# Seven products of 256 columns in place of eight, in five of the eight MLP blocks

## The chip, the cores and the metric

The kernel runs on one core of one Trainium2 chip. The metric is the device time of one execution in microseconds (us). An execution here is one call on the whole input: 2048 tokens, both layers.

## The reference

Two layers, each with a linear-attention block and an MLP, on one sequence of S = 2048 tokens with D = 448 features; 16 heads of 28; hidden size F = 1792. All in float32.

```python
x = x + A(layernorm(x), wqkv, wo)      # phi(q), phi(k) = where(t > 0, t + 1, exp(t)) + 1e-6
                                       # o = phi(q) @ (phi(k).T v) / (phi(q) . sum phi(k) + 1e-6), then @ wo
x = x + (gelu(layernorm(x) @ w1 + b1) @ w2 + b2)
# both lines twice, with the same weights
```

The change touches the product `layernorm(x) @ w1` (2048 x 448 times 448 x 1792) and what feeds it.

## The kernel before

**Precision.** Every large product is made in the type fp32r from split operands: a float32 value is written as hi + lo, and a product takes three matmuls, hi x hi, hi x lo and lo x hi. Of the 448 input features, 384 make three full chunks of 128 rows; the last 64 are laid twice into one chunk, so that hi and lo of the weight stand above one another, and need two matmuls in place of three. A product over all features thus takes 3 x 3 + 2 = 11 matmuls.

**Stages.** Each layer has a first phase over 16 tiles of 128 tokens (layer norm, projections to k and q, sums for attention), a short middle part, and four blocks of 512 tokens. A block goes over 14 chunks i of 128 hidden features. For each, `mlp1` makes the product with w1 (11 matmuls of 512 tokens, L1011), then gelu on ScalarE (L1013), the cast to hi on ScalarE (L1016) and the low part on VectorE (L1017). `mlp2` (L1040 to L1042) multiplies gelu's hi and lo with w2: four token tiles times three matmuls of 448 columns, added up in four PSUM banks over all 14 chunks; then VectorE adds the sum to x (L1045) and SP stores it (L1047).

**Order.** All instructions stand in an order written by hand; each engine runs its own in order. `mlp1` of chunk i + 1 stands ahead of `mlp2` of chunk i, and of the next block's first chunk ahead of the last `mlp2`. Between them `behind` puts the preparation of the next block: the tuples `PLAN_0`, `PLAN_1` and `PLAN` name for each chunk which steps go there. Tokens: `ld`, `g` loads; `z`, `p`, `q`, `o` the attention output of one token tile (`o` is `oc_mm`, L948 to L952, 11 matmuls, and `o_ln`, L969 and the layer norm's statistics); `n` the normalisation and a transpose in 32x32 squares on VectorE (L308); `sx` and `lx` a way through DRAM that completes the transpose; `x` (`m_part`, L354 and L355) the split of a piece of the MLP's operand, the cast on ScalarE and the low part on VectorE.

**Buffers.** w1 and w2 are split once, hi and lo, and stay in SBUF: `w1h`, `w1l`, `w1x`, `w2h`, `w2l`. They are loaded and split piece by piece in layer 0 (`bg_pieces`, `background`: cast on ScalarE, L419, L422, L430; low part on GpSimd, L420, L423, L431), w1 and four chunks of w2 during the first phase and the rest of w2 during the first block. The transposed operand of a block lies in XH and XL, two buffers each. PSUM has eight banks: "h" (2) for hp, "acc" (4) for the sums of `mlp2`, "m" (2) for op and others.

**Queues.** Nearly all DMAs are issued by SP, in program order; where one waits, those behind it wait too.

Of the kernel before, what the change touches and what calls it, by code (L numbers as in the profile page):

```python
# [22 lines left out]
def linear_attn_mlp_kernel(  # L23
# [22 lines left out]
    NG = D // G  # L46
    TL = D - 64
    LAYERS = 2

# [151 lines left out]
    w2l = wts.tile([128, NF, D], F32R, name="w2l")  # L201

# [29 lines left out]

    class Block:
        def __init__(self, key):
            at = APART if key[0] == "a" else 0
            self.rows = key[0] == "m"
            self.hi = work.tile([128, 2048], F32R, name="XH", tag="XH", bufs=2)
            self.lo = work.tile([128, 2112], F32R, name="XL", tag="XL", bufs=2)[:, at:at + 2048]

        def pieces(self, t):  # L240

            if self.rows:
                return tuple(x.rearrange("p (c t n) -> p t c n", c=4, t=4)[:, t] for x in (self.hi, self.lo))
            s = slice(t * 512, (t + 1) * 512)
            return self.hi[:, s], self.lo[:, s]

        def moving(self, x, c):

            return x[:, c * 512:(c + 1) * 512]

        def still(self, x, t, c):

            return x[:, (t * 4 + c) * 128:(t * 4 + c + 1) * 128]
# [71 lines left out]
    def half_square(name, j):  # L325

        if j >= 2:
            return t512("AB"[j - 2], 2, name)
# [8 lines left out]
    def turn_one(x, key, j):  # L337
# [4 lines left out]
                      x[:, TL:D].rearrange("p (m n) -> p m n", n=32)[:, None].to_broadcast([128, 2, 2, 32]))  # L342

# [19 lines left out]
    def proj(name, key, j, o=None, cs=range(4), at=(3, 6, 9, 11)):  # L363
# [3 lines left out]
        if len(cs) == 4:  # L367
            w = [wkq[name, c] for c in range(3)]
            his = [(b.still(b.hi, j, c), p) for c in range(3) for p in w[c]] + [(b.still(b.hi, j, 3), wkq[name, 3])]
            los = [(b.still(b.lo, j, c), w[c][0]) for c in range(3)] + [(b.still(b.lo, j, 3), wkq[name, 3])]  # L370
# [3 lines left out]
        for c in cs:  # L374
            if c < 3:
                hi, lo = wkq[name, c]
                pe.matmul(o, b.still(b.hi, j, c), hi, start=(c == 0), stop=False)
                pe.matmul(o, b.still(b.hi, j, c), lo, start=False, stop=False)
                pe.matmul(o, b.still(b.lo, j, c), hi, start=False, stop=False)
            else:  # L380
                pe.matmul(o, b.still(b.hi, j, 3), wkq[name, 3], start=False, stop=False)
                pe.matmul(o, b.still(b.lo, j, 3), wkq[name, 3], start=False, stop=True)
# [11 lines left out]

    def bg_pieces():
        n = 0
        both = []

        def stage():
            nonlocal n  # L400
            n += 1
            if n <= LATE:
                k = (n - 1) // 2
                if k % 2 == 0 or k > 5:
                    return t512("xn", 2, "stg")[:, :D]

                if n % 2:
                    both.append(half("stg"))
                return both[-1][:, n % 2 * 512:][:, :D]
            return t448(f"W{5 + n % 2}", 1, "stg")  # L410

        for fc in range(4):
            sl = slice(fc * D, (fc + 1) * D)
            for c in range(4):
                s = stage_piece(w1[:, sl], c, sp, stage())

                def go(c=c, s=s, sl=sl):
                    if c < 3:
                        act.copy(w1h[:, c, sl], s)  # L419
                        pool.tensor_tensor(w1l[:, c, sl], s, f(w1h[:, c, sl]), op=OP.subtract)  # L420
                    else:
                        act.copy(w1x[:, sl], s)  # L422
                        pool.tensor_tensor(w1x[64:128, sl], s[64:128], f(w1x[64:128, sl]), op=OP.subtract)  # L423
                yield go
        for i in range(NF):
            s = stage()
            sp.dma_start(s, w2[i * 128:(i + 1) * 128, :])

            def go(i=i, s=s):
                act.copy(w2h[:, i], s)  # L430
                pool.tensor_tensor(w2l[:, i], s, f(w2h[:, i]), op=OP.subtract)  # L431
            yield go
# [4 lines left out]
    def background(n, m=NF):  # L437

        for g in bg_wait[:m]:
            bg_wait.pop(0)()  # L440
        for _ in range(n):
            g = next(bg, None)
            if g is not None:
                bg_wait.append(g)


# [45 lines left out]
    def stage_s(l, t):  # L492
        xn = xns.pop((l, t))
        h = t512("A", 2, "xnh", F32R)
        lo = t512("B", 2, "xnl", F32R, APART)
# [81 lines left out]
    def product(name, t, c, p):  # L577
# [8 lines left out]
        pe.matmul(o, b.still(b.lo if p == "l" else b.hi, t, c), w, start=(n == 0), stop=(n == 11))  # L586
# [57 lines left out]
    def stage_g(l, t, acc, mid=lambda: None):  # L644
# [618 lines left out]
```

## Time and profile before

| what | value |
|---|---|
| median of 3 runs | 864.18 us (864.15 to 867.68) |
| profiled execution | 864.72 us |
| its span | 863.0 us |
| busy: TensorE, its weight loads | 857.2 us (99%), 768.1 us (89%) |
| busy: VectorE, ScalarE, GpSimd | 493.0, 352.8, 211.6 us |
| matmuls in L1011 | 1232 of 512 columns |
| moved by DMA | 97.89 MB |

The span is the time between the first and the last instruction that the profiler recorded. Busy times of TensorE's rows overlap, since its instructions are pipelined: the mean duration of a matmul is longer than the distance between two starts. "acc", "h" and "m" are names of PSUM banks, not columns of the profile.

### The profile page before, as it was taken

The numbers are of one execution on the slowest core, as the hardware profiler recorded it, in microseconds if no ns is written. First come the engines' busy times: TensorE is split into PE (matmuls) and PEld (weight loads), VectorE is DVE, ScalarE is ACT, GpSimd is POOL, SyncE is SP. The second block draws the span as 40 slices with busy tenths as digits, with TensorE's granted clock in tenths as the row PEclk, the third lists the DMA queues.
The fourth block names the chain that finished last, engine by engine and source line by source line (L and its number), as shares of the span: only waits on it lengthen the run. The fifth ranks groups of instructions, "written<-read, shape, count | busy, mean of one in ns | idle before, by whom it ended". The sixth has DMA issues, their size and how long they took to land.

```text
span 863.0 us, 11715 instructions
## 1 busy us (share of the span) xinstructions
PE 857.2 (99%) x4155; PEld 768.1 (89%) x4155; DVE 493.0 (57%) x962; ACT 352.8 (41%) x635; POOL 211.6 (25%) x244
## 2 busy tenths in 40 slices
PE   9999999999999999999999999999999999999998
PEld 8999988888888888888899998988888888888887
DVE  7888586559456443236477876764664383533112
ACT  7676655323323322333356565633232233233231
POOL 3576612235013012012222343120310140140000
PEclk9999999999999999999999999999999999999999
DMA  5485647633313402051146442462332423111001
GB/s 171 150 270 180 206 108 217 191 113 121 123 61 123 140 0 98 1 182 49 49 150 188 164 130 96 146 204 81 123 113 78 140 74 111 49 49 43 1 1 43
DMA packets 68681, 97.89 MB, mean 113 GB/s; under 512 B 9488, under 2 KB 62864, under 8 KB 68624
## 3 DMA queue, kind: packets, MB, share of 16 engines
q1 hardware_dynamic: 67872, 96.76, 35.0%
q8 instruction: 32, 0.52, 0.3%
q10 hardware_dynamic: 752, 0.41, 0.2%
q14 instruction: 25, 0.20, 0.1%
HBM read 57.74 MB, written 36.18 MB: 109 GB/s over the span
## 4 chain that ended last, share of the span: by engine, by line
PE 90%; DVE 4%; DMA 3%; issue 1%; ACT 1%; POOL 1%; SPq 0%; DVEq 0%; ACTq 0%; POOLq 0%
PE hp L1011 32%; PE y L1041 10%; PE y L1040 10%; PE y L1042 10%; PE psq L372 5%; PE G L658 5%; PE psk L372 5%; PE op L949 2%; PE op L948 2%; PE op L950 2%; DMA sp<-sq_a 1%; PE op L938 1%; PE op L937 1%; PE op L939 1%; PE kvp L824 1%
## 5 line engine op out<-in xcount | busy, mean ns | idle before, releaser
L1017 DVE TENSOR_TENSOR gl<-g,gh 128x512 fp32r<-128x512 f32 x112 | 83.2, 743 | 293.0 <-ACT gh L1016 293.0
L1013 ACT ACTIVATE g<-hp,b1s 128x512 f32<-128x512 f32 x112 | 77.1, 689 | 400.8 <-PE hp L1011 400.8
L1041 PE MATMUL y<-w2l,gh 128*128 128x448 f32 x447 | 163.6, 366 | 0.0
L1040 PE MATMUL y<-w2h,gh 128*128 128x448 f32 x447 | 162.0, 362 | 0.0
L1042 PE MATMUL y<-w2h,gl 128*128 128x448 f32 x447 | 160.0, 358 | 0.0
L1011 PE MATMUL hp<-XH,w1h 128*128 128x512 f32 x336 | 130.7, 389 | 0.0
L1011 PE MATMUL hp<-XH,w1l 128*128 128x512 f32 x336 | 130.7, 389 | 0.0
L1011 PE MATMUL hp<-XL,w1h 128*128 128x512 f32 x336 | 130.1, 389 | 0.0
L216 POOL TENSOR_TENSOR brs<-bve,mhalf 128x1 f32<-128x1 f32 x55 | 34.2, 622 | 258.5 <-DVE bve L215 250.8
L1040 PEld LDWEIGHTS y<-w2h,gh 128*128 128x128 f32 x447 | 83.7, 187 | 9.4
L1041 PEld LDWEIGHTS y<-w2l,gh 128*128 128x128 f32 x447 | 83.9, 188 | 7.0
L1042 PEld LDWEIGHTS y<-w2h,gl 128*128 128x128 f32 x447 | 84.0, 188 | 5.0
L1011 PEld LDWEIGHTS hp<-XL,w1h 128*128 128x128 f32 x336 | 63.1, 188 | 13.1
L1011 PEld LDWEIGHTS hp<-XH,w1h 128*128 128x128 f32 x336 | 63.0, 187 | 10.7
L1011 PEld LDWEIGHTS hp<-XH,w1l 128*128 128x128 f32 x336 | 63.1, 188 | 9.9
L1016 ACT CAST gh<-g 128x512 fp32r<-128x512 f32 x112 | 69.6, 621 | 3.6
L372 PE MATMUL psk<-wk,XH 128*128 128x448 f32 x210 | 61.8, 364 | 0.0
L372 PE MATMUL psq<-wq,XH 128*128 128x448 f32 x196 | 57.0, 365 | 0.0
L497 POOL TENSOR_TENSOR xnl<-x,xnh 128x384 fp32r<-128x384 f32 x32 | 35.0, 1094 | 73.5 <-ACT xnh L496 60.3
L355 DVE TENSOR_TENSOR XL<-sp,XH 128x512 fp32r<-128x512 f32 x58 | 47.2, 825 | 5.7 <-ACT XH L354 5.7
L883 POOL TENSOR_TENSOR pz<-pq,zb 128x448 f32<-128x448 f32 x24 | 28.2, 1174 | 89.9 <-DVE dn L894 61.8
L658 PE MATMUL G<-kh,xnh 128*128 128x448 f32 x128 | 46.7, 367 | 0.0
(194 smaller groups left out, 1500.2 us busy)
## 6 DMA issues: line engine op xcount, KB each, us to landing
x<-in_A_x_dram SPq DMA_DIRECT2D x32, 224.0 KB, 3.9
pq_d<-eq SPq DMA_DIRECT2D x32, 224.0 KB, 2.5
pq<-pq_d SPq DMA_DIRECT2D x32, 224.0 KB, 3.6
x<-x_d SPq DMA_DIRECT2D x32, 224.0 KB, 3.9
sq_a<-sq SPq DMA_DIRECT2D x13, 512.0 KB, 2.9
sp<-sq_a SPq DMA_DIRECT2D x52, 128.0 KB, 2.9
sq_q<-sq SPq DMA_DIRECT2D x12, 512.0 KB, 2.6
sp<-sq_q SPq DMA_DIRECT2D x48, 128.0 KB, 2.8
```

The lines of the kernel that those rows point to most:

```text
L216: pool.tensor_tensor(rs, ve, mhalf, op=OP.pow)
L355: eng.tensor_tensor(lo.rearrange("p c (i n) -> p c i n", n=32), x, f(h), op=OP.subtract)
L372: pe.matmul(o, x, p, start=(i == 0), stop=(i == 10))
L497: pool.tensor_tensor(lo[:, :TL], xn[:, :TL], f(h[:, :TL]), op=OP.subtract)
L658: pe.matmul(acc[c], w, k, start=first and c not in others[0], stop=last and c not in others[1])
L1011: pe.matmul(hp, w, r, start=(k == 0), stop=(k == len(made) - 1))
L1013: act.activation(g, hp, AF.Gelu_apprx_tanh, bias=b1s[:, i:i + 1])
L1016: act.copy(gh, g)
L1017: dve.tensor_sub(gl, g, f(gh))
L1040: pe.matmul(acc[j], gh[:, s], w2h[:, i], start=first, stop=False)
L1041: pe.matmul(acc[j], gh[:, s], w2l[:, i], start=False, stop=False)
L1042: pe.matmul(acc[j], gl[:, s], w2h[:, i], start=False, stop=stop)
```

## The change

In five of the eight blocks (the third and fourth of layer 0, the second to fourth of layer 1) the product with w1 is made by Strassen's scheme in Winograd's form. A block's 512 tokens are halved, the features are halved (two chunks each) and a pair of hidden chunks is halved: eight products of quarter size become seven, of sums. The operand's sums S1 to S4 are made by GpSimd in place in the transposed tiles and then split like any piece (seven pieces a block in place of four). Products 1, 6, 7 and 4 add up in one bank of "h", 5 and 3 in one half of a bank of "m", 2 in its other half; ScalarE copies three of them to SBUF on the way, and VectorE adds three times. Products 1, 5, 6 and 7 take six matmuls of 256 columns, 2, 3 and 4 take five.

The sums of w1 are made once, in layer 0's first blocks (`seven_pair`: four subtractions and an addition on GpSimd, casts on ScalarE, low parts on VectorE, 13 DMAs a pair of chunks). w1's split parts no longer stay in SBUF: all blocks, the three old ones too, fetch them from DRAM, pair by pair, into two tiles with two buffers each. XH and XL become rings of nine pieces. The other three blocks keep their 11 matmuls of 512 columns; their operand is now read in four stretches of 128. `mlp2`'s matmuls are the same in number and shape, in another order.

```diff
+    SEVEN = {(0, 2), (0, 3), (1, 1), (1, 2), (1, 3)}
...
-    w1h = wts.tile([128, 3, F], F32R, name="w1h")
-    w1l = wts.tile([128, 3, F], F32R, name="w1l")
-    w1x = wts.tile([128, F], F32R, name="w1x")
...
+    def fetch_a(p, seven=True):
+        w = w1a[seven, p] = work.tile([128, 12 * 128], F32R, name="w1a", tag="w1a", bufs=2)
+        if seven:
+            sp.dma_start(f(w[:, :512]), w1c_d[p][:, :512])
+            sp.dma_start(f(w[:, 512:]), w1t_d[p][:, :1024])
+        else:
+            sp.dma_start(f(w[:, :1024]), w1c_d[p][:, :1024])
+
+    def fetch_b(p, seven=True):
+        w = w1b[seven, p] = work.tile([128, 13 * 128], F32R, name="w1b", tag="w1b", bufs=2)
+        sp.dma_start(f(w[:, :768]), w1c_d[p][:, 1024:])
+        if seven:
+            sp.dma_start(f(w[:, 768:]), w1t_d[p][:, 1024:])
...
+    def seven_pair(p):
...
+        pool.tensor_tensor(t1, t3, t1, op=OP.subtract)
+        pool.tensor_tensor(t3, t2, t3, op=OP.subtract)
+        yield
+        pool.tensor_tensor(t2, t2, t1, op=OP.subtract)
+        pool.tensor_tensor(t4, t4, t2, op=OP.subtract)
+        yield
+        high = temp("th", F32R)
+        act.copy(high, top)
...
-        (0, 5): "qp K s kp X kh v9 a10 kl n10 G bg Q ld sp",
+        (0, 5): "qp K s kp X kh v9 a10 kl n10 G sp bg Q ld",
...
+    PRODUCTS = {1: ("a", (0, 1, 2, 3), "A11"), 5: ("a", (4, 6, 5, 7), "S1"), 6: ("a", (8, 10, 9, 11), "S2"),
+                2: ("b", (0, 4, 2), "A12"), 3: ("b", (1, 5, 3), "S4"), 7: ("b", (6, 8, 7, 9), "S3"), 4: ("b", (10, 12, 11), "A22")}
...
+        def product(self, n):
+            w, at, name = PRODUCTS[n]
...
+            made = [(u[0], h[0]), (u[1], h[0]), (u[0], x[0])]
+            made += [(u[2], h[1]), (u[3], h[1]), (u[2], x[1])] if n in (1, 5, 6, 7) else [(u[2], h[1]), (u[2], x[1])]
+            if n in (1, 6, 7, 4):
+                first = n == 1
+                self.X = bank("h", 2, "hx") if first else self.X
+                o = self.X[:, :256]
+            else:
+                first = self.HB is None
+                self.HB = bank("m", 2, "hy") if first else self.HB
+                o = self.HB[:, 256:] if n == 2 else self.HB[:, :256]
...
+        def keep_2(self):
+            self.s2 = self.small("s2")
+            act.copy(self.s2, self.x())
...
+        def c12(self):
+            dve.tensor_tensor(self.s2, self.s2, self.y(), op=OP.add)
+
+        def rest(self):
+            self.gelu(21, self.x())
+            self.gelu(12, self.s2)
+            self.high(12)
+            self.high(21)
+            self.low(12)
+            self.low(21)
...
     LATER = (
         "n3 sx1 ld1 ld2",
         "lx1 ld3 z0",
-        "x0 p0 z1",
-        "x1 p1 sq0 z2",
-        "x2 p2 z3 lq0",
-        "x3 p3 sq1",
-        "",
-        "lq1",
+        "p0 z1",
+        "c1 c3 p1 sq0 z2",
+        "x0 x1 p2 z3 lq0",
+        "c2 c4 p3 sq1",
+        "x2 x3 x4",
+        "x5 lq1",
     )
...
+    def step(l, b, k, tr):
+        c = todo.pop(0)
+        n = len(ahead) - len(todo) + 1
+        before = open_.pop(0)
+        q = quarters(before)
+        c.product(1)
+        c.keep_1()
+        if (before.l, before.b) not in SEVEN:
+            q[0]()
+            c.product(2)
+            c.c11()
+            c.product(6)
+            c.keep_2()
+            c.product(5)
+            c.keep_5()
+        else:
+            c.product(5)
+            c.keep_5()
+            before.rest()
+            q[0]()
+            c.product(2)
+            c.c11()
+            c.product(6)
+            c.keep_2()
+        fetch(held_a, fetch_a, n)
...
+        if k == 0:
+            token_piece(l, b, 6)
+        c.g11()
+        q[1]()
+        c.product(7)
+        c.c22()
+        c.low(11)
...
+        beside(l, b, 2 * k, tr)
+        q[2]()
...
+        q[3]()
+        c.low(22)
+        c.product(3)
+        c.product(4)
+        c.c12()
+        beside(l, b, 2 * k + 1, tr)
...
+        fetch(held_b, fetch_b, n)
+        open_.append(c)
```

A step is one pair of chunks: its seven products stand between the four quarters of the pair before it (11, 22, 12, 21 by token half and hidden half, six matmuls of 448 columns each). `beside` calls `behind` with the plan's tokens for the step's two chunks; `c1` to `c4` are the operand's sums, `x0` to `x5` its pieces. `more`, left out, takes `seven_pair` one `yield` further; it is called in layer 0's first three blocks.

More of the change, by code (lines that the diff above doesn't have):

```diff
@@ L392, in phi @@
         return into
-    def bg_pieces():
[L396 to L424, printed above, removed]
-        for i in range(NF):
[L426 to L432, printed above, removed]
@@ L447, in linear_attn_mlp_kernel, with sevens @@
+    def sevens():
+        for p in MADE:
+            yield from seven_pair(p)
+        yield
+    seven = sevens()
     xns, split, ks = {}, {}, {}
@@ L701, in linear_attn_mlp_kernel @@
     PRE = 5
-    BG = [0, 1] + [2] * 6 + [1] * 7 + [0]
-    LATE = sum(BG)
     loaded = {0: 3}
@@ new lines, in linear_attn_mlp_kernel, with fetch, quarters @@
+    todo, open_ = [Pair(*c) for c in ahead], []
+    held_a, held_b = ([(False, 0), (False, 1)] for _ in range(2))
+    def fetch(held, get, n):
+        if n < len(ahead):
+            l, b, p = ahead[n]
+            key = ((l, b) in SEVEN, p)
+            if key not in held:
+                get(p, key[0])
+                held.append(key)
+                del held[0]
+    def quarters(c):
+        if (c.l, c.b) not in SEVEN:
+            return [lambda i=i, js=js: mlp2(c.l, c.b, i, js) for i, js in
+                    ((NF - 2, range(4)), (NF - 1, (0, 1)), (NF - 1, (2, 3)), (NF - 1, ()))]
+        first, last = (c.p == turn_of(c.l, c.b)[i] for i in (0, -1))
+        return [lambda q=q: quarter(c, q, first, last) for q in (11, 22, 12, 21)]
@@ L1132, in linear_attn_mlp_kernel, with last_step @@
+    def last_step():
+        while open_:
+            c = open_.pop(0)
+            c.rest()
+            for q in quarters(c):
+                q()
     table(AF.Exp)
```

520 lines of the change are left out of this document (404 added, 116 removed), and 6 rows, old and new, of tables (ORDER, STEPS).

## The prediction

> **What bounds the kernel now.** I read the page's busy table and its slices first, then TensorE's matmuls grouped by line and shape, then single matmuls in order of time, then the windows that fit the blocks, and last the groups of ScalarE, VectorE and GpSimd.
>
> ```profile
> span 863.0 us, 11715 instructions
> PE 857.2 (99%) x4155; PEld 768.1 (89%) x4155; DVE 493.0 (57%) x962; ACT 352.8 (41%) x635; POOL 211.6 (25%) x244
> PEclk9999999999999999999999999999999999999999
> PE 90%; DVE 4%; DMA 3%; issue 1%; ACT 1%; POOL 1%; SPq 0%; DVEq 0%; ACTq 0%; POOLq 0%
> L1011 PE MATMUL hp<-XH,w1h 128*128 128x512 f32 x336 | 130.7, 389 | 0.0
> L1011 PE MATMUL hp<-XH,w1x 128*128 128x512 f32 x112 | 43.6, 389 | 0.0
> 286.30:363.60 77.30, 77.30 (x367) 68.62 (x366) 28.37 (x54) 22.71 (x36) 7.68 (x8) 1.00 0.19 63
> 788.30:859.40 71.10, 71.10 (x338) 62.74 (x337) 14.13 (x23) 18.34 (x28) 0.00 (x0) 1.00 0.04 15
> ```
>
> TensorE is the clock of this kernel: 99% busy, 90% of the chain, full clock in every slice, and no idle time before any L1011 group. In the two windows, which are two of the eight MLP blocks (layer 0's third, layer 1's last; in the columns PE, PEld, DVE, ACT, POOL, clock, DMA share, GB/s), the other engines are busy for 8 to 29 of 71 to 77 us. So what the change is worth is first a sum over matmuls, and what one costs is the distance between starts, since busy times overlap.
>
> ```profile
> 599.81 0.39 PE L1011 MATMUL hp<-XH,w1h 128*128 128x512 f32 x1
> ...
> 602.30 0.36 PE L948 MATMUL op<-wq,qh 128*128 128x448 f32 x1
> ```
>
> ```profile
> 788.31 0.39 PE L1011 MATMUL hp<-XH,w1h 128*128 128x512 f32 x1
> ...
> 790.81 0.36 PE L1040 MATMUL y<-w2h,gh 128*128 128x448 f32 x1
> ```
>
> ```profile
> 854.82 0.36 PE L1042 MATMUL y<-w2h,gl 128*128 128x448 f32 x1
> ...
> 858.62 0.26 PE L1032 MATMUL yh<-w2h,gh 128*128 128x224 f32 x1
> 858.72 0.28 PE L1033 MATMUL yh<-w2l,gh 128*128 128x224 f32 x1
> ...
> 859.17 0.27 PE L1034 MATMUL yh<-w2h,gl 128*128 128x224 f32 x1
> ```
>
> Eleven 512-wide matmuls take 2.49 us in one place and 2.50 us in the other: 4.99 / 22 = 226.8 ns each. Nineteen 448-wide take 3.80 us: 200 ns. The difference, 26.8 ns for 64 columns, is 0.42 ns a column, and the line through both has a fixed part of about 13 ns. The 224-wide ones at the very end start 0.45 / 4 = 112.5 ns apart in their steady part, where the line would give 106.
>
> **The first product, term by term.** A pair of feature chunks takes 2 x 11 = 22 matmuls of 512 columns today. The scheme's seven products take 4 x 6 + 3 x 5 = 39 matmuls of 256. Five blocks of seven pairs are 35 pairs: 770 wide matmuls leave (770 x 0.2268 = 174.6 us), 1365 narrow ones come. No group of 256 columns is in the trace. The line gives 200 - 192 x 0.42 = 119.4 ns, and I take 120. The low bound is the 112.5 ns of the 224-wide row, as if that were a floor below which no width matters; the high bound is that row plus 32 columns, 112.5 + 13.4 = 126 ns. I stay with 120 because 112.5 looks like a second limit, the weight load's, which these rows show:
>
> ```profile
> 858.73 0.19 PEld L1034 LDWEIGHTS yh<-w2h,gl 128*128 128x128 f32 x1
> ...
> 858.84 0.19 PEld L1032 LDWEIGHTS yh<-w2h,gh 128*128 128x128 f32 x1
> ...
> 859.07 0.19 PEld L1034 LDWEIGHTS yh<-w2h,gl 128*128 128x128 f32 x1
> ```
>
> Loads of 0.19 us start 0.11 us apart, so they overlap, and one matmul per 0.113 us (0.34 / 3) is what they allow; 120 is above it, so the columns decide again. The sum: 1365 x 0.120 = 163.8, a gain of 10.8 us. At 112.5 it is 153.6 and 21.0; at 126 it is 172.0 and 2.6. The change breaks even at 174.6 / 1365 = 127.9 ns. All depends on 8 ns a matmul.
>
> The Trainium skill speaks against the change here: "Perfetto Trace Analysis", Identifying the Most-Contended Engine, says that weight loads' busy share, not matmul's, tells how near TensorE is to its limit. By it the 595 more loads at 188 ns would add 112 us to a row that is 89% busy, more than the span has room for. The three load rows above contradict this, since they overlap.
>
> The second product keeps its count: a pair was 2 x 12 matmuls of 448 and is four quarters of 6. Its cost stays 24 x 0.200 = 4.8 us, and a step of the new loop is 39 x 0.120 + 4.8 = 9.5 us, against 9.8.
>
> **What has to hide in a step.** ScalarE and VectorE get more and shorter instructions.
>
> ```profile
> L1013 ACT ACTIVATE g<-hp,b1s 128x512 f32<-128x512 f32 x112 | 77.1, 689 | 400.8 <-PE hp L1011 400.8
> L1016 ACT CAST gh<-g 128x512 fp32r<-128x512 f32 x112 | 69.6, 621 | 3.6
> L281 ACT CAST XH<-tp 128x512 fp32r<-128x512 f32 x4 | 2.3, 572 | 0.9 <-PE tp L269 0.9
> L290 ACT CAST XH<-tp 128x256 fp32r<-128x256 f32 x4 | 1.4, 368 | 0.1
> L1017 DVE TENSOR_TENSOR gl<-g,gh 128x512 fp32r<-128x512 f32 x112 | 83.2, 743 | 293.0 <-ACT gh L1016 293.0
> L292 DVE TENSOR_TENSOR XL<-tp,XH 128x256 fp32r<-128x256 f32 x4 | 1.6, 422 | 0.4 <-ACT XH L290 0.2
> ```
>
> Halving a ScalarE copy from 512 to 256 columns saves 572 - 368 = 204 ns. So a pair's ScalarE work goes from 2 x (689 + 621) = 2.6 us to three kept products (368 each), four gelus (689 - 204 = 485) and four casts (621 - 204 = 417): 4.7 us of 9.5. VectorE goes from 1.5 to 7 x 0.42 = 3.0 us. Neither is a bound; their order is what counts. The tightest place: product 7 adds onto the bank that keep_2 has to copy first. Between product 6 and product 7 stands one quarter, 6 x 0.200 = 1.2 us. On ScalarE's queue ahead of keep_2 are keep_1, keep_5 and, once the loop runs, the two gelus and two casts of the pair before: 2 x 368 + 2 x 485 + 2 x 417 = 2.5 us. Product 1 ends at 0.72 us in the step and product 6 at 0.72 + 0.72 + 1.2 + 0.6 + 0.72 = 3.96. A matmul's result is there about 0.17 us after its slot (366 ns shown against 200). Started at about 0.9, with a wait for product 5, ScalarE is through by about 3.9; keep_2 runs to some 4.6 and product 7 is due at 5.16. It holds with 0.5 us over. I cost it at nothing; without that margin each 0.1 us late costs 35 x 0.1 = 3.5 us.
>
> **Stalls that I do cost.** First, the products' other bank comes from the same two banks as attention's output op. Where two of these fall in one step (o0 and o1, o2 and o3), the second needs the bank that c12 still reads, and c12 stands on VectorE behind the first one's chain.
>
> ```profile
> L210 DVE BATCH_NORM_STATS2 bst<-x 128x6 f32<-128x448 f32 x4 | 2.5, 628 | 0.1
> L969 DVE TENSOR_TENSOR x<-op,x 128x448 f32<-128x448 f32 x4 | 2.5, 624 | 0.6
> L308 DVE STREAM_TRANSPOSE sq<-xm 128x384 f32<-128x384 f32 x4 | 2.3, 578 | 0.1
> L228 DVE TENSOR_SCALAR xm<-x,bmv,brs 128x448 f32<-128x448 f32 x4 | 2.0, 504 | 0.0
> ```
>
> These four with about half a microsecond of small ones and low22 (0.42) make 3.3 us, against two quarters and products 3 and 4, 2.4 + 1.2 = 3.6. With c12's own 0.42 the second op is 0.2 to 0.7 us late: 0.45 in each of two steps in three blocks (those that prepare another), 2.7 us; bounds 0 and twice that.
>
> Second, each of the two passages from an old block to a new one: ScalarE there has one gelu and one cast (1.3 us), four operand pieces (4 x 0.62) and then keep_1, some 4.3 us after the last wide matmul, while product 6 is due after product 1, twelve second products and product 2, 0.72 + 2.4 + 0.6 = 3.7. I take 0.8 us twice, 1.6; bounds 0 and 4.
>
> At the layers' ends the last pair's gelus and casts need about 2.2 us under two quarters of 2.4; nothing there. The operand's three more pieces a block and four sums on GpSimd (below 1.4 us each by the row below) lie behind blocks where these engines are idle for over half of the time.
>
> **Layer 0 and the DMA.** Weights of the first product no longer stay in SBUF.
>
> ```profile
> q1 hardware_dynamic: 67872, 96.76, 35.0%
> 30.00:60.00 30.00, 30.00 (x152) 27.82 (x152) 26.71 (x57) 21.70 (x43) 20.61 (x25) 1.00 0.65 209
> 134.00:145.00 11.00, 11.00 (x52) 9.50 (x51) 6.08 (x12) 6.05 (x10) 2.75 (x2) 1.00 0.79 250
> 156.00:167.00 11.00, 11.00 (x53) 9.76 (x53) 6.23 (x10) 4.59 (x8) 3.29 (x3) 1.00 0.77 221
> L883 POOL TENSOR_TENSOR pz<-pq,zb 128x448 f32<-128x448 f32 x24 | 28.2, 1174 | 89.9 <-DVE dn L894 61.8
> ```
>
> 96.76 MB in 35.0% of 863 us is 320 MB per ms of full use, so the 25 blocks of 64 KB (1.6 MB) that a pair fetches are 5.1 us of DMA in a step of 9.5 to 10.3, some 50% beside the 0.19 of the block in the first fence: about 0.7, and each fetch is issued a whole step ahead. SP is held at a fetch until product 6 or 4 has read the old tile; what queues behind it is the next plan's loads, of a later step. It is tighter in layer 0: 6.4 MB of stores in the first phase (20 us of DMA over some 84, on top of 0.65), and in the first block, at 0.77 to 0.79 for its first 33 us, three fetches and the first sums' transfers, 3 to 4 MB or about 11 us more. That reaches 100%, so loads land a few microseconds late. Behind them on ScalarE stand casts of pieces, and behind these the gelus; the two banks of hp cover about 2.5 us of that. Bounds 0 to 8 us; I take 0.7, since those loads are planned two chunks (over 10 us) ahead.
>
> **Sum.** 864.7 (the profiled execution, 1.7 over its span) - 10.8 + 2.7 + 1.6 + 0.7 = 858.9. The median shown is 0.5 lower, so I expect 858.4.
>
> **Rivals.**
> (1) All is hidden: 864.2 - 10.8 = 853.4. For it: no idle time before L1011 today. Against: the shared bank. Chance 0.17.
> (2) The forecast, 855.5 to 859.8: 0.38.
> (3) No change, 860 to 868: the price is 125 to 126 (a gain of 2.6 to 4.0, eaten by the stalls: 864.2 - 3.3 + 5 = 865.9), or the DMA of layer 0 takes its upper 8 us (858.4 + 7.3 = 865.7). Chance 0.29.
> (4) Slower: keep_2 gates product 7. It decides as soon as ScalarE is later than its margin by (10.8 + 4.3) / 35 = 0.43 us a step, that is 0.9 us later than my count. At 0.9 us of stall a step: 858.4 + 31.5 = 890; at 0.6, 879. For it: in-order ScalarE stands in the step's middle with seven instructions and can be held by a late transfer or sum. Against: 4.7 us of work in 9.5. Chance 0.12.
> (5) The floor of 112.5 ns holds at 256 columns: 858.4 - 10.2 = 848. "TensorE: Matmul & The Clock Gate" in the Trainium skill, Back-to-back issue gap, would have N / 2.4 + 2.5 = 109 ns, thus 1365 x 0.109 = 149 and a gain of 26. The 448- and 512-wide rows, 11 ns above that rule each, speak against it. Chance 0.03.
> (6) Weight loads don't overlap at this width: 1365 x 0.188 = 256.6, time 858.4 + 92.8 = 951. The yh rows speak against it; 0.01.
>
> **The numbers.** Changes under 0.5%, 4.3 us, can't be told from none. Faster, below 859.9: 0.17 + 0.38 + 0.03 = 0.58, less 0.02 for stalls near the border, 0.56. Slower, above 868.5: 0.13 with (6), and 0.01 from the end of (3), 0.14. Same 0.30. The range goes from 851.5, a little under the full gain, to 867, where the first half of (3) and the DMA case end; the likeliest case's own is 855.5 to 859.8.
>
> **What would show it.** Narrow matmuls 119 to 121 ns apart inside a product; 0.2 to 0.7 us of TensorE idle ahead of every second op; short idles at product 6 of the first pair; none at product 7; DMA at 0.6 to 0.8 in the new blocks. Wrong would be: over 124 ns, idle before product 7 in most steps, or tens of microseconds of idle in layer 0's first 240 us.

## The result, and the profile after

The changed kernel takes 907.25 us (median of 4 runs, 904.54 to 910.5) beside 864.36 us for the kernel before (864.15 to 867.68): the ratio is 1.0488, with a 95% interval from 1.044 to 1.0537. It is 4.9% slower. The profiled execution took 904.54 us, 1.7 us over its span.

From the page of the changed kernel: span, busy times, the granted clock in 40 slices, the DMA queue, the chain by engine, and one group of the narrow matmuls (busy us, mean ns, idle us before it and what ended it).

```profile
span 902.8 us, 13895 instructions
...
PE 867.3 (96%) x4750; PEld 795.4 (88%) x4750; DVE 573.0 (63%) x1180; ACT 428.8 (47%) x907; POOL 269.6 (30%) x304
...
PEclk9999899989999979999999999999999999999999
...
q1 hardware_dynamic: 112894, 179.15, 61.4%
...
PE 75%; DMA 9%; DVE 8%; SPq 3%; ACT 2%; issue 2%; POOL 1%; DVEq 0%; ACTq 0%; POOLq 0%
...
L1174 PE MATMUL hx<-XH,w1a 128*128 128x256 f32 x280 | 53.8, 285 | 0.6 <-ACT s L1190 0.6
```

TensorE's share of the chain fell from 90% to 75%; DMA rose from 3% to 9%, VectorE from 4% to 8%. The queue moved 179.15 MB in place of 96.76. The clock has three slices below 9. So matmuls no longer set the end everywhere; windows tell where. From the windows of the changed kernel (stretch, length, then busy us and count of PE, PEld, DVE, ACT, POOL, the granted clock, the DMA share, GB/s):

```profile
60.00:104.00 44.00, 34.28 (x146) 29.94 (x145) 25.03 (x52) 20.67 (x38) 18.53 (x26) 0.88 0.71 238
...
175.00:186.00 11.00, 7.34 (x34) 6.01 (x32) 2.69 (x7) 3.10 (x6) 3.98 (x6) 0.96 0.92 274
186.00:197.00 11.00, 9.39 (x34) 7.83 (x35) 6.90 (x12) 3.18 (x6) 4.23 (x4) 0.73 0.87 261
...
312.00:330.00 18.00, 13.30 (x62) 11.74 (x61) 12.70 (x20) 7.85 (x17) 8.69 (x7) 0.72 0.67 207
...
396.00:475.00 79.00, 79.00 (x504) 75.40 (x503) 47.34 (x107) 44.44 (x105) 13.88 (x15) 1.00 0.67 221
...
592.00:620.00 28.00, 25.28 (x118) 21.73 (x116) 17.29 (x34) 9.53 (x16) 4.62 (x4) 1.00 0.85 256
...
671.00:690.00 19.00, 17.32 (x110) 15.88 (x109) 14.04 (x27) 11.26 (x26) 3.47 (x3) 1.00 0.67 236
```

Once the new blocks run (396 to 475) TensorE is full. It is idle in the first phase, in the first block, at the first entry into a new block (312 to 330), in layer 1's first block (592) and at the second entry (671).

The first phase ends with the first kvp matmul. Its row in the view of that tile (duration ns min/median/max, first and last start) says 104.3 us in the kernel before and 122.9 in the changed one:

```profile
L824 PE MATMUL kvp<-gt,stg x64: 258/262/262, 104.3 to 532.0; 128*112 128x112 f32 x64
```

```profile
L934 PE MATMUL kvp<-gt,stg x64: 258/262/263, 122.9 to 565.9; 128*112 128x112 f32 x64
```

The table is made the same way, from starts of single matmuls: a block runs from its first matmul with w1 to the next one's. "Stall" adds up, over a stage, how much the distances between starts exceed 200 ns after a 448-wide matmul, 226.7 after 512 and 120 after 256; in the kernel before it is 1.7 us in the first phase and 0.0 in every block. (The eight matmuls on `mp` in each layer's middle part are left out of it. At each of the two passages from an old block to a new one 12 second products change sides of the mark, 2.4 us, so of the stages on both sides of a passage only the stall compares.)

| stage | before, us | after, us | stall after, us |
|---|---|---|---|
| first phase, layer 0 | 104.3 | 122.9 | 20.3 |
| layer 0: first, second block (old) | 75.0, 77.4 | 83.7, 75.4 | 8.8, 0.5 |
| layer 0: third block (new) | 77.4 | 84.8 | 9.6 |
| fourth (new) and the next first phase | 165.3 | 166.2 | 1.1 |
| layer 1: first block (old) | 75.0 | 78.1 | 5.6 |
| layer 1: second, third, fourth (new) | 77.4, 77.4, 70.9 | 79.9, 76.4, 72.0 | 4.7, 1.3, 0.8 |

All stalls come to 54.0 us against 3.3: with 10.8 us less of matmuls, 54.0 - 3.3 - 10.8 = 39.9, and the last matmul starts 898.9 - 859.2 = 39.7 us later.

### The profile page after: what moved, and what is told of

The parts are those of the page before. It is cut to its first block, busy times and chain, and to the rows that moved or that the text cites. A ratio compares the mean times of both kernels' runs of the same rounds, so it can differ in the third digit from the quotient of the medians.

```text
span 902.8 us, 13895 instructions
## 1 busy us (share of the span) xinstructions
PE 867.3 (96%) x4750; PEld 795.4 (88%) x4750; DVE 573.0 (63%) x1180; ACT 428.8 (47%) x907; POOL 269.6 (30%) x304
## 3 DMA queue, kind: packets, MB, share of 16 engines
q1 hardware_dynamic: 112894, 179.15, 61.4%
## 4 chain that ended last, share of the span: by engine, by line
PE 75%; DMA 9%; DVE 8%; SPq 3%; ACT 2%; issue 2%; POOL 1%; DVEq 0%; ACTq 0%; POOLq 0%
PE hx L1174 10%; PE hp L1257 8%; PE hy L1174 7%; PE y L1317 6%; PE y L1316 6%; PE y L1318 6%; PE psq L390 5%; PE G L768 5%; PE psk L390 4%; PE y L1276 3%; PE y L1275 2%; PE y L1277 2%; DMA sp<-sq_a 2%; DMA low<-in_B_w_dram 2%; DMA sq_a<-sq 2%; PE op L1062 2%
## 5 line engine op out<-in xcount | busy, mean ns | idle before, releaser
L1215 DVE TENSOR_TENSOR gl<-g,gh 128x256 fp32r<-128x256 f32 x140 | 66.3, 494 | 59.7 <-ACT gh L1211 59.0
L1259 ACT ACTIVATE g<-hp,b1s 128x512 f32<-128x512 f32 x42 | 28.9, 688 | 125.0 <-PE hp L1257 121.4
L1263 DVE TENSOR_TENSOR gl<-g,gh 128x512 fp32r<-128x512 f32 x42 | 32.2, 766 | 70.1 <-ACT gh L1262 70.0
L1202 ACT ACTIVATE g<-s,b1s 128x256 f32<-128x256 f32 x105 | 53.5, 509 | 46.0 <-DVE s L1226 29.8
L1318 PEld LDWEIGHTS y<-w2h,gl 128*128 128x128 f32 x279 | 52.4, 188 | 5.5 <-DVE gl L1215 1.6
L1317 PEld LDWEIGHTS y<-w2l,gh 128*128 128x128 f32 x279 | 52.8, 189 | 2.7
L1211 ACT CAST gh<-g 128x256 fp32r<-128x256 f32 x140 | 53.4, 405 | 3.3
L1174 PE MATMUL hx<-XH,w1a 128*128 128x256 f32 x280 | 53.8, 285 | 0.6 <-ACT s L1190 0.6
L390 PE MATMUL psk<-wk,XL 128*128 128x448 f32 x120 | 45.2, 377 | 9.2 <-DVE XL L373 9.2
L1257 PE MATMUL hp<-XH,w1a 128*128 128x512 f32 x168 | 51.4, 390 | 0.8 <-ACT XH L372 0.8
```

The source lines that it names most:

```text
L390: pe.matmul(o, x, p, start=(i == 0), stop=(i == 10))
L1174: pe.matmul(o, w, r, start=(first and k == 0), stop=(k == len(made) - 1), skip_group_check=True)
L1202: act.activation(g.rearrange("p (u i n) -> p i u n", u=2, i=4), x.rearrange("p (i u n) -> p i u n", u=2, i=4), AF.Gelu_apprx_tanh, bias=b1 ...
L1211: act.copy(self.h[:, s], g)
L1215: dve.tensor_sub(lo, g, f(hi))
L1257: pe.matmul(hp, w, r, start=(k == 0), stop=(k == len(made) - 1))
```

## The experiments

Each run's time stands beside that of the kernel before on the same chip. In the expectations, Q says that the first phase loses its time to the stores, by their bytes and their place in SP's queue; E, the rival to Q, that the engines' added casts and subtractions cost the time; H, formed when Q had missed, that the first phase loses it to one load that runs on two DMA engines; G, that GpSimd waits in order for a late load of w1's sums; N, that a 448-wide matmul costs more by itself once narrow ones have run.

**No store of the split weights.** Only the first pair's split parts are stored, and all pairs fetch these; w1's sums are still made for every pair.

```diff
-    w1c_d = [dram([128, 14 * 128], F32, f"w1c_d{p}") for p in range(NP)]
+    w1c_d = [dram([128, 14 * 128], F32, "w1c_d")] * NP
...
-            unsaved.append((w1c_d[p][:, :1024], f(w[:, :1024])))
+            if p == MADE[0]:
+                unsaved.append((w1c_d[p][:, :1024], f(w[:, :1024])))
```

> Leaves out 12 of the 14 stores of w1's split parts in layer 0's first phase (only the first pair's is stored, and every pair fetches that one, so the outputs are not the reference's); casts, subtractions, loads and fetches stay. Theory Q (SP's one ordered queue and the rings behind it: transfers that are put ahead of the round trips through DRAM make the transposed operands late): the first phase, 122.9 us in the changed kernel and 104.3 before (start of kvp), falls to 108 or less, the total to about 889. Theory E (the new casts and subtractions on ScalarE, VectorE and GpSimd make them late): the phase stays at 118 or more, the total at 900 or more. Blocks after it are the same in both.

It took 897.87 us (before: 863.8). The first phase ended at 118.6 us: 4.3 us less, with 14 us of loss left. The stores aren't what costs most, and Q missed; the phase came out where E had it, at 118 or more, but what E names isn't the cause either, as the split load below shows.

**The sums' transfers without their arithmetic.** `seven_pair` keeps every DMA; its work on GpSimd, ScalarE and VectorE is left out.

```diff
-        pool.tensor_tensor(t1, t3, t1, op=OP.subtract)
-        pool.tensor_tensor(t3, t2, t3, op=OP.subtract)
...
-        high = temp("th", F32R)
-        act.copy(high, top)
```

> Keeps all DMAs of w1's sums in layer 0's first blocks, in number, size and place, and leaves out their arithmetic on GpSimd, ScalarE and VectorE (unsummed values are stored, so the outputs are not the reference's). In the changed kernel the first block takes 83.7 us (75.0 before) and the third 84.8. Theory Q: the first block stays over 80, since its stall follows a late transfer; the third falls to 76 to 78, since there GpSimd's instructions wait in order for a late load and hold the operand's sums; total about 896. Theory E: both fall, the first to 77 or less, total about 887.

It took 893.86 us (863.8). The third block fell from 84.8 to 77.6 us, and its stall from 9.6 to 2.4; the first block's stall fell from 8.8 to 6.4. Both blocks came out where Q had them. So what holds the third block is the sums' instructions on the engines, by their work or by what they wait for, and not the traffic. In the timeline of GpSimd of the changed kernel (start, us, what; in brackets idle time before it) this is seen at work:

```profile
302.20 0.74 POOL L516 TENSOR_TENSOR top<-top 128x256 f32<-128x256 f32 x1 [5.88 <-issue]
303.02 0.74 POOL L517 TENSOR_TENSOR top<-low,top 128x256 f32<-128x256 f32 x1
303.72 1.78 POOL L1129 TENSOR_TENSOR S<-sp 128x512 f32<-128x512 f32 x1
```

GpSimd sits idle for 5.88 us at the first subtraction of a pair's sums (L516), and the operand's sum S (L1129), which the third block needs, is queued behind it. Here the profile doesn't name what the subtraction waits for ("issue"). In the run without stores, whose instructions are the same at this place, it names it: the raw load of w1's rows.

```profile
298.99 0.74 POOL L518 TENSOR_TENSOR top<-top 128x256 f32<-128x256 f32 x1 [6.87 <-DMA top<-in_B_w_dram]
```

The chain of the changed kernel (start, us, what) goes on from that wait, over some 13 us of VectorE's work, to the stalled product:

```profile
298.74 3.47 issue
...
303.72 1.79 POOL S L1129
...
317.60 1.53 DVE XL L1138
319.13 2.87 DVE XL L1142 x3
...
322.38 1.65 PE hy L1174 x6
```

With the arithmetic left out, the window of the same entry has 17.19 us of TensorE in 18 in place of 13.30, at more DMA (0.94), not less:

```profile
312.00:330.00 18.00, 17.19 (x108) 15.85 (x107) 11.79 (x23) 11.01 (x26) 1.38 (x2) 1.00 0.94 308
```

**Stores in every second step alone.**

```diff
-        begin(BG[t])
+        begin(BG[t], t % 2 == 0)
```

Where the second argument is false, the unsaved parts wait for the next step.

> The changed kernel complete, with the stores of w1's split parts issued only in the steps of layer 0's first phase in which no transposed tile is stored (even steps), so that none stands directly ahead of such a store on SP's queue. Same bytes, same arithmetic. Theory Q by order: the first phase falls from 122.9 to 104 to 111 us, total about 892. If it is the bytes and not the order: 119 or more. Theory E: no change, 121 to 124.

It took 900.9 us (863.8), the first phase 119.4 us: 3.5 us of 18.6. That is above the 111 that Q by order allows: the order of the stores decides little.

**Fetches behind the plan's loads.**

```diff
-                fetch(held_a, fetch_a, n)
-                fetch(held_b, fetch_b, n)
             if b == 0 and i == 0:
                 next(moves, None)
             beside(l, b, i, tr)
+                fetch(held_a, fetch_a, n)
+                fetch(held_b, fetch_b, n)
```

> The changed kernel complete, with one order changed: in the three old blocks the fetch of the next pair's weights is issued behind the chunk's other loads and stores and behind the second half of the moves of the attention matrix, not ahead of them. Theory Q: layer 1's first block, where no sums are made, falls from 78.1 to 73 to 75 us and layer 0's first from 83.7 to 77 to 81; total about 895. Theory E: layer 1's first block stays at 77 or more.

It took 904.98 us (863.8). In layer 0 the stall moved: 7.9 us in the first block (8.8), 6.5 in the second (0.5), 5.1 in the third (9.6). Layer 1's first block had 2.5 in place of 5.6, but the runs without stores and with stores in even steps, whose code is the changed kernel's there, had 2.5 and 2.0. So this run decides nothing on that block.

**The load in two pieces.** After Q, the waits of the first phase pointed at one load, which fills 128 rows with two copies of w1's last 64 rows.

```diff
-        sp.dma_start(x[:, 256:], w1[TL:, p * 256:(p + 1) * 256][None].to_broadcast([2, 64, 256]))
+        for h in range(2):
+            sp.dma_start(x[h * 64:(h + 1) * 64, 256:], w1[TL:, p * 256:(p + 1) * 256])
```

> The changed kernel complete, with one transfer of the first phase split: the last 64 rows of w1, laid twice into a tile by one DMA whose source repeats them, are loaded by two DMAs of 64 rows. Same bytes, one more issue for each pair. Theory H (packets of that load ran on two of the 16 DMA engines, about 3.6 us each time, and every transfer behind them on these two engines was late): the first phase, 122.9 us in the changed kernel, 118.6 without the stores and 104.3 before, falls to 105 to 111, the total to about 890. Rival (bytes or the engines' added work): it stays at 117 or more, the total over 898.

It took 893.94 us (864.18), and the first phase 111.3 us, just over H's 111 and far from the rival's 117; the total is 4 us over H's 890. The same bytes by the same queue, in two DMAs in place of one, save 11.6 of the 18.6 us. In the view of waits from 20 to 123 us (who waited for what: us, times, longest), first the changed kernel, then this one:

```profile
ACT w1b L467 <- DMA low<-in_B_w_dram: 18.4, 6, 5.6
```

```profile
ACT w1b L468 <- DMA low<-in_B_w_dram: 4.8, 2, 3.8
```

In its tile's view the first kvp is at 111.3:

```profile
L935 PE MATMUL kvp<-gt,stg x64: 258/262/262, 111.3 to 556.5; 128*112 128x112 f32 x64
```

A count over the packets of the two traces shows what the load does: mean number of the 16 DMA engines that were busy, by packet size, microsecond by microsecond.

```
changed kernel   62 us: 1024 B  2.1   1792 B  1.4   3072 B 10.7
                 63 us: 1024 B  2.1   1792 B 11.3   3072 B  1.2
                 64 us: 1024 B  2.1   1792 B  6.5   4096 B  7.8
                 70 us: 1024 B  2.2   nothing else
first phase (20 to 108 us), time with 1.7 to 2.4 engines on packets of 1024 B:
before 0.0 us   changed 17.0 us   load in two pieces 1.0 us
```

Two engines carry that load, alone at 70 us, while the other 14 move next to nothing. What hangs on it shows in ScalarE's timeline of the changed kernel (idle time before it and its releaser in brackets): the cast of the loaded piece waits for 5.18 us, and the first step of attention's exponential (L406) stands behind it.

```profile
66.98 0.62 ACT L467 CAST w1b<-low 128x512 fp32r<-128x512 f32 x1 [5.18 <-DMA low<-in_B_w_dram]
67.51 0.54 ACT L406 ACTIVATE eq<-psq 128x448 f32<-128x448 f32 x1
```

The chain of the changed kernel runs through the same load, 7.62 us from its issue, and on through the store that SP gives out only then; the read back of the turned square (`sp<-sq_a`) is queued behind that store.

```profile
59.29 7.62 DMA low<-in_B_w_dram
...
66.97 8.99 DMA w1c_d<-w1a
```

**All blocks old, weights fetched.** With the load in two pieces, and no block by the scheme: no sums, the old plan.

```diff
-    SEVEN = {(0, 2), (0, 3), (1, 1), (1, 2), (1, 3)}
+    SEVEN = set()
...
-    seven = sevens()
+    seven = iter(())
```

> One part of the change alone: w1's parts are stored in DRAM and fetched pair by pair in all eight blocks, but all blocks use the old product (11 matmuls of 512 columns) and no sums are made; the load of the last 64 rows is split as in the run before. It computes the reference. If streaming cost nothing it would be at 864 to 866. Theory H with full DMA engines in the blocks that follow the attention's matrix: first phase 105 to 111, first block of layer 0 77 to 80, of layer 1 75 to 78 (75.0 before for both), total 870 to 877. Rival (the sums and not the streaming cost layer 0's first block its time): both first blocks at 75 to 76, total 866 to 870.

It took 877.84 us (864.18): 13.7 us of loss without any of the scheme. The first phase took 111.7 us and the first block 80.9; every other block took what it takes before, to 0.2 us, layer 1's first block too (75.0, no stall). So a weight that comes from DRAM costs a steady old block nothing, and what layer 1's first block loses comes with the new blocks and their plan.

**No stores and no sums, the load in two pieces.** Only the first pair is stored and summed; the new blocks run.

```diff
-        for p in MADE:
+        for p in MADE[:1]:
             yield from seven_pair(p)
```

> The split load, and of w1's parts and sums only the first pair's are stored and made; all pairs fetch these (so the outputs are not the reference's). Fetches and all products stay. The five new blocks are then free of the preparation. Theory: first phase 104 to 107, layer 0's first block 76 to 80, its third about 77 (84.8 in the changed kernel), layer 1's first 74 to 76, total 868 to 873. If the new blocks alone lose time, the third block stays over 81 and the total over 877.

It took 878.17 us (864.18).

```profile
L937 PE MATMUL kvp<-gt,stg x64: 258/262/263, 105.0 to 539.2; 128*112 128x112 f32 x64
```

The first phase ended at 105.0 us, so the stores cost 111.3 - 105.0 = 6.3 us once the load is mended. The third block's stall was 2.4 us, as without the arithmetic. What was left over the kernel before lies in the first block (82.7 us) and layer 1's first (77.8, a stall of 5.3). The five new blocks together were only some 1.1 us shorter than the old ones, of the 10.8 that matmuls save.

**Four blocks by the scheme**, so that the sums have three old blocks to hide in (load in two pieces).

```diff
-    SEVEN = {(0, 2), (0, 3), (1, 1), (1, 2), (1, 3)}
+    SEVEN = {(0, 3), (1, 1), (1, 2), (1, 3)}
...
-        if (2 if b == 0 else 0) <= i < (NF if b == 0 else 9):
+        if (9 if b == 0 else 0) <= i < (NF if b < 2 else 9):
...
-        if l == 0 and b < 2:
+        if l == 0 and b < 3:
```

> A version for the time, complete: the split load; layer 0's third block keeps the old product, so four blocks use the new one; w1's sums are made from the tenth chunk of layer 0's first block to its third block. Theory: first phase 105 to 111, layer 0's first block 78 to 81, second and third 77 to 79, total 874 to 882; the sums no longer stand ahead of the operand's sums on GpSimd. Rival (sums cost as much wherever they stand): total 885 or more.

It took 883.77 us (864.18), between the theory's 882 and the rival's 885, and 10.2 less than with the load alone. Most of the sums now lie in the second and third block, whose stalls are 1.9 and 0.2 us, and the first new block, now layer 0's fourth, loses little: that stage stalls for 1.7 us and took 166.9 us. The first block still took 80.0.

**Narrow matmuls alone.** The kernel before, with layer 1's last block made in halves of 256 columns: same weights, same order, no scheme.

```diff
-        for k, (w, r) in enumerate(made):
-            pe.matmul(hp, w, r, start=(k == 0), stop=(k == len(made) - 1))
+        for h in halves:
+            for k, (w, r) in enumerate(made):
+                pe.matmul(hp[:, h], w, r[:, h], start=(k == 0), stop=(k == len(made) - 1))
```

> The kernel before, complete, with one edit: in layer 1's last block each of the first product's matmuls of 512 columns is made as two of 256 (22 narrow ones a chunk in place of 11). It measures the narrow price by itself, without sums, fetches or a new order. At 120 ns the block's 308 narrow matmuls cost 308 x 0.120 - 154 x 0.2267 = 2.05 us more. Theory N (narrow matmuls also leave the 448-wide ones behind them at 204.6 ns in place of 200.0, as all five new blocks of the changed kernel show): 168 x 4.6 ns = 0.8 us on top, the 448-wide matmuls of this block 204 to 205 ns apart, the span longer by 2.8 us. Rival (the 204.6 ns come from the new kernel's other traffic): 200 ns, the span longer by 2.05 us.

It took 867.17 us (863.95), and its last block 73.7 us in place of 70.9. From its timeline of TensorE:

```profile
790.53 0.37 PE L1042 MATMUL y<-w2h,gh 128*128 128x448 f32 x1
...
792.99 0.28 PE L1013 MATMUL hp<-XH,w1h 128*128 128x256 f32 x1
...
794.91 0.28 PE L1013 MATMUL hp<-XL,w1h 128*128 128x256 f32 x1
```

Sixteen narrow matmuls take 1.92 us, 120 ns each; twelve of 448 columns take 2.46 us, 205 ns each, where the same twelve take 200 in the kernel before. Over the block the means are 119.9 and 204.7. N held, with no new wait anywhere near.

**All repairs together**: load in two pieces, stores in even steps, fetches late, four blocks.

> A version for the time, complete, with all the orders tried together: the split load, the stores in even steps, the late fetch, four new blocks and the sums from layer 0's first block's tenth chunk on. If their gains add up: first phase 105 to 109, layer 0's first block 77 to 81, layer 1's first 75 to 76, total 872 to 878, slower than before by 1.0 to 1.6%. If the stores merely move the wait, the first phase stays at 111 and the total at 880 or more. Faster than before would need the new blocks to gain more than the 1.3 us each that they show.

It took 888.09 us (median; 886.46 to 889.6) against 863.95: a ratio of 1.0268, interval 1.0246 to 1.029. It is 4.3 us worse than the one run of the four blocks without the two changes of order. The first phase took 111.0 us, as the second reading had it, so with the load mended the even steps gain nothing, and the stalls of the first two blocks were 8.2 and 6.8 us in place of 5.1 and 1.9. Repairs that each seemed worth a few microseconds don't add up.

**Sums paused in the third block's preparation** (load in two pieces).

```diff
-        if (2 if b == 0 else 0) <= i < (NF if b == 0 else 9):
+        if i < (NF, 7, 9, 0)[b]:
```

> The changed kernel complete with the split load, and the making of w1's sums started two chunks earlier in layer 0's first block and paused from the eighth chunk of its second (not the tenth), so that none of it is left on GpSimd's queue when the operand's sums of the third block are due. Theory G (GpSimd waits in order for a late load of w1's sums and holds the operand's sums): the third block, 85.6 us with the split load alone and 77.6 without the sums' arithmetic, falls to 77 to 80, total 885 to 889. Rival (VectorE's and ScalarE's share of the sums, not their place): it stays over 82.

It took 893.94 us (863.95), what it took with the load alone. The third block took 80.0 us, at the end of what G allows and below the rival's 82: its stall fell from 10.4 to 4.9 us. But the first block's rose from 10.4 to 15.6, so the total missed. The loss of the sums goes where the sums go.

**No fetch in the first block.** As with all blocks old, but layer 0's first block uses the weights of two pairs over and over.

```diff
+            if (l, b) == (0, 0):
+                (w1a if get is fetch_a else w1b)[False, p] = (w1a if get is fetch_a else w1b)[False, p % 2]
+                return
```

> The run with streaming alone (old product in all blocks, split load, no sums) once more, without the fetches in layer 0's first block: its pairs 2 to 6 use the weights of pairs 0 and 1 over again (so the outputs are not the reference's); all other blocks fetch. Layer 0's first block took 80.9 us there and 75.0 before. Theory (these fetches, 0.9 MB each, stand ahead of the attention's round trip in full DMA queues): it falls to 75 to 76.5, the total from 877.8 to 872 to 874. Rival (the block's other transfers, or the order of its plan): it stays at 79 or more.

It took 872.94 us (863.63). Windows of the first block, first of the kernel with all blocks old, then of this one:

```profile
145.00:220.00 75.00, 71.53 (x328) 62.24 (x327) 46.37 (x83) 24.77 (x43) 27.63 (x24) 0.98 0.78 228
```

```profile
145.00:220.00 75.00, 75.00 (x356) 66.49 (x355) 51.78 (x92) 27.57 (x48) 29.79 (x26) 1.00 0.53 164
```

The DMA share falls from 0.78 to 0.53 and the first block takes 75.0 us, without a stall: the fetches cost it all of its 5.9 us, there and only there, beside the loads of w2 that the block has anyway. Whether by their bytes or by their place in SP's queue, this run doesn't separate; in the changed kernel the later place alone took 0.9 us off that block's stall.

No version tried is faster than the kernel before.

## Why the prediction was wrong

**The narrow price was right.** 120 ns was taken and 119.9 to 120 measured, in the changed kernel and alone. In the changed kernel's timeline of TensorE the six matmuls from 889.71 to 890.42 took 0.71 us:

```profile
888.48 0.37 PE L1316 MATMUL y<-w2h,gh 128*128 128x448 f32 x1
...
889.71 0.40 PE L1174 MATMUL hx<-XH,w1b 128*128 128x256 f32 x2
...
890.42 0.37 PE L1316 MATMUL y<-w2h,gh 128*128 128x448 f32 x1
```

The gain of 10.8 us in matmuls with w1 is there. The formula N / 2.4 + 2.5 of "TensorE: Matmul & The Clock Gate" in the Trainium skill (Back-to-back issue gap), which that section calls the isolated gap and not that of a stream, would have 109 ns. The stream in these rows doesn't follow it.

**"Its cost stays 24 x 0.200" was wrong in size.** The same rows have six 448-wide matmuls in 889.71 - 888.48 = 1.23 us, 205 ns each. At 4.6 to 5 ns over, 168 second products in each of five blocks cost 3.9 to 4.2 us, and attention's op in these blocks a few tenths: 40% of the gain. The narrow matmuls alone do it in the old kernel.

**keep_2 was right but for one step.** The rival that it gates product 7 would have been the slower side; the kernel is slower, but not by that.

```profile
L1174 PE MATMUL hx<-XH,w1b 128*128 128x256 f32 x245 | 49.8, 286 | 0.6 <-ACT s L1194 0.6
```

Behind keep_2 (L1194) TensorE waited once in the whole kernel, for 0.6 us at 687 us, in the second step of layer 1's second block; there the gelus ahead of keep_2 had waited for VectorE. The chain's products 1 come 9.59 us apart, (453.71 - 367.44) / 9, and the step was predicted at 9.5:

```profile
367.44 1.32 PE hx L1174 x11
...
453.71 1.32 PE hx L1174 x11
```

The shared bank, put at 2.7 us, cost next to nothing: the steady new blocks stall for 0.8 to 1.3 us, and some 0.8 of that is the 204 ns.

**The passages were too cheap, and more is lost behind one.** Each was put at 0.8 us. The first stalls for 2.4 us without the sums' arithmetic, less 0.8 of slower 448-wide matmuls some 1.6. The second block of layer 1 stalls for 4.7 to 5.3 us in every run that has it as a new block, in the changed kernel at three places besides the 0.8: 1.6 us at the passage, 0.8 at keep_2 in the next step, 1.5 at 745 us, near its end. In the chain of the changed kernel VectorE's low parts of the operand's pieces at the passage, and two attention rows near the end, stand ahead of what TensorE waits for:

```profile
673.39 1.25 DVE XL L1142
...
674.95 1.28 DVE XL L1142 x2
...
676.62 0.98 PE hy L1174 x6
```

```profile
740.35 1.19 DVE pq L1017
...
744.34 1.50 DVE pq L1017
...
746.63 1.76 DVE gl L1215 x2
```

I had counted ScalarE's queue at the passage; it was VectorE's that was last. The two passages cost some 3.2 us, twice the 1.6 of the sum and within its bound of 4. The 0.8 and the 1.5 behind the second passage stood in no term: I had said that neither engine is a bound, but from 726 to 749 us the chain runs on VectorE but for 2.4 us.

**The step that failed is "layer 0 and the DMA": 0.7 us, bounds 0 to 8.** It measured 18.6 in the first phase, 8.8 in the first block and some 7.2 in the third, 34.6 us; the last of these comes with the arithmetic of w1's sums, which no term had. I had summed bytes and taken the share of 16 engines that they fill. For the first phase that gives some 0.9 (0.65 and 20 of 84 us), so no loss; the trace has 0.71 from 60 to 104 us, below it, and yet 15 us of that phase's stall lie there. For the first block I had said that the share would reach 100%; it was 0.87 to 0.92 from 175 to 197 us, where most of that block's stall lies. Three things were not in that sum.

- One load uses two engines: 11.6 us. "DMA: Bandwidth & Descriptors" in the Trainium skill (Why a DMA increments its semaphore by 16 and not by 1) says that a DMA is spread over the largest number up to 16 that divides the slowest dimension of both its sides. The source here is 2 x 64 x 256, which gives two, and the packets agree with 2.1 to 2.2.
- In these kernels each engine and queue takes its work in order. On ScalarE a late load holds attention's exponentials behind its cast, on SP the next store and the read behind that, and on GpSimd, in the third block, the operand's sum.
- I covered late loads with "planned two chunks ahead". In the first phase nothing is ahead: a step's square is stored, read back turned, and used at once, and from 45 to 107 us that read took 6.2 us to land (median of 16), against 3.0 in the kernel before and 3.7 with the load in two pieces. In the first block the weights' fetches alone, 5.9 us, undo the cover, at a share of 0.78 over the block.

The stores, which I had as 20 us of DMA, cost 6.3 us once the load was mended, and 4.3 before: two causes on one path.

**Layer 1's first block wasn't priced at all.** It stalls for 5.6 us in the changed kernel and for 2.0 to 5.6 in the runs with the new plan, for 0.0 in the two with the old one, whose fetches are the same where it stalls. In the chain of the changed kernel attention's transposed tile lands late, behind a row of fetches and loads on SP:

```profile
608.16 3.89 DMA sq_q<-sq
...
613.38 6.48 DMA sp<-sq_q
```

The new plan asks for the first output op one chunk earlier. That this chunk is the cause agrees with all runs, but it wasn't changed by itself, and why the loss differs from run to run stays open.

**Where the 39.9 us are.** Matmuls with w1: -10.8. Slower 448-wide ones: +4.2. First phase: +18.6 (11.6 the load, 6.3 the stores, 0.7 other). First block: +8.8 (5.9 fetches, the rest with the sums; with the sums in the same place the runs have 8.8 to 11.3, with one pair of them 7.8, with their transfers alone 6.4). Third block, without the slower matmuls: +8.7 (7.2 arithmetic, 1.5 passage). Layer 1's first: +5.6, its second: +3.9 (1.6 passage, 0.8 keep_2, 1.5 near its end). Other blocks: +0.9. With every cost of layer 0 but its passage, and that of layer 1's first block, gone, the sum would be -10.8 + 4.2 + 1.5 + 3.9 + 0.9 = -0.3: even then, no change that can be measured. Had I taken the DMA at its upper 8, I should still have said "no change": the bound itself was wrong, since it came from the same mean share.

## What to carry to other kernels

A mean DMA share says how many bytes fit, not when a transfer lands: in a phase where each step's store, reload and use follow one another, count each new DMA by the time to its landing, by the engines that its shape gives it, and by what is queued behind it on the issuing engine. Read every new load's outermost dimension; a copy made by a broadcast in front can put a small load on two engines. A saving inside a tight loop has to be weighed against the whole loop, since here the unchanged matmuls beside the narrow ones took back 40% of it.

## What the runs showed of the hardware

Matmuls of 448 columns, which start 200 ns apart in the kernel before, start 204 to 205 ns apart in a block whose other matmuls have 256 columns, between two of their own kind too. The same matmuls with half the columns at a time show it with nothing else changed. Its cause is open; no wait stands in the profile.

In the windows with the long stalls the mean granted clock fell to 0.73 (186 to 197 us) and 0.72 (312 to 330 us). In the changed kernel's record of the granted clock it is 0.5 five times between 72 and 626 us, for 3.4 to 10.2 us each and 30.7 us in all. In the longest of these, 318 to 328 us, which began inside a wait of 3.4 us, the chain has 448-wide matmuls 0.37 us apart:

```profile
324.41 0.37 PE y L1276
324.78 0.37 PE y L1277
325.15 0.37 PE y L1275
```

So a stall there costs more than its own length, and part of what is put down above to fetches, sums and load is this lower clock: matmuls that start 1.6 to 1.95 times their usual distance apart add up to some 3.7 us in the first phase and 2.9 in the third block.
